# Attention with a projected sequence, then a maxout feed-forward layer: k of batch 1 turned by the DMA crossbar

## The chip, the cores and the metric

The kernel runs on one core of one Trainium2 chip. A core has five engines with instruction streams of their own: TensorE (PE in the profile; its weight loads are PEld), VectorE (DVE), ScalarE (ACT), GpSimd (POOL) and SyncE (SP). They share an on-chip buffer (SBUF), a buffer for matmul results (PSUM, eight banks of 512 fp32 values in each of 128 partitions) and 16 DMA engines. The metric is the device time of one execution in microseconds; the median of several runs is compared.

## The reference, cut to what matters

```python
# batch 8, heads 8, sequence 1024, head size 64, projected length 64
k_proj = np.einsum('ks,bhsd->bhkd', E, k)
v_proj = np.einsum('ks,bhsd->bhkd', F, v)
scores = np.matmul(q, k_proj.transpose(0, 1, 3, 2)) / 8
attn = np.exp(scores - max);  attn = attn / sum(attn)
x = np.matmul(attn, v_proj)            # then 8192 tokens x 512
h = np.maximum(np.maximum(x @ w1, x @ w2), x @ w3)    # 512 -> 768
out = h @ w_out                                      # 768 -> 512
```

The layer after the attention is most of the work: for each batch of 1024 tokens it has two chunks of 512 tokens, with 72 matmuls of 128x128 by 128x512 for the maxout and 24 for the way down.

## The kernel before

One instruction stream for each engine is written by hand as a list of steps. A step is one group of matmuls of the feed-forward layer: `l1` (four matmuls into one bank, for one of the three weights and one of six column blocks) or `down` (six matmuls into one bank). `at(slot, f)` puts a piece of the next batch's attention behind step `slot` of the present batch. Pieces run in the order in which they are listed, once their step is reached.

```python
def kv(b, bank=AB, crossbar=True):
    ...  # 8 + 8 matmuls: k projected into the lower half of the bank, v into the upper
    nc.scalar.copy(out=kp2[i][:, :, :, 0, :], in_=...)           # ScalarE
    nc.scalar.copy(out=vp2[b % 3][KP:P], in_=kv_v[:, 1])
    nc.vector.tensor_copy(out=kp_[:, :, 1:], in_=...)            # VectorE: three more copies of k
    nc.vector.tensor_copy(out=vp2[b % 3][0:KP], in_=kv_v[:, 0])
    if crossbar:
        nc.sync.dma_start_transpose(out=kpT[i]..., in_=kp2[i]...)

def kp_turn(b):                      # the same turn by TensorE, 16 transposes
    for h in range(H):
        for f in range(2):
            nc.tensor.transpose(out=psb[:, AB + h // 4, x:x + KP], ...)
    for j in range(2):
        (nc.vector.tensor_copy if j else nc.scalar.copy)(out=kpT[i][:, 4 * j:4 * j + 4]..., in_=psb[:, AB + j, ...])
```

`scores` takes `kpT` as weights and the turned q (`qT`, turned by VectorE in `q_flip`), and then gives two exponentials to ScalarE. The sums over the projected length and the product with v are small matmuls in quarter tiles (`quads`), each with two adjacent PSUM banks as its target. Banks 4 to 7 belong to the attention (`AB = 4`), banks 0 to 3 go round among the feed-forward groups (`fbank`). Some products borrow an adjacent pair from that ring (`fpair`).

```python
def sums(b):
    for ch in range(2):
        quads(b, ch, AB + 2 * ch, lambda rows, g: ones[rows, :])
    log(0)

def av3(b):
    lo = fpair()
    for f, ch, bank in ((0, 0, lo), (1, 0, AB), (0, 1, AB + 2)):
        av(b, f, ch, bank)
    norm(b, 0, 0, lo)

def av1(b):
    lo = fpair()
    av(b, 1, 1, lo)
    norm(b, 1, 1, lo)

def l1(b, ch, c, jt, i):
    bank = fbank()
    ...  # four matmuls
    if i == 0:   nc.scalar.copy(out=h1s[jt % 2], in_=ps[:, bank, :])                    # L225
    elif i == 1: nc.vector.tensor_tensor(out=m12[jt % 2], ..., in1=h1s[jt % 2], op=ALU.max)  # L227
    else:        nc.vector.tensor_tensor(out=hT[c % 2][:, jt, :], ..., in1=m12[jt % 2], op=ALU.max)  # L229

def load_behind_turn(b, order="qkv", q_of=None):
    nc.gpsimd.tensor_copy(out=seen, in_=kpT[(b - 1) % NB][:, 0, 0, 0:1])   # waits for the turn of batch b - 1
    ...
    for c in order:
        load(b, ...)
```

In the first two batches the pieces stand at these steps. Steps 17 to 34 of batch 0 are the 18 `l1` groups of chunk 1, steps 35 to 38 its four `down` groups; step 1 of batch 1 is the first `l1` of chunk 2.

```python
if b == 0:
    at(8, q_up0, slice(4, 8))
    for x in ((k, k_t), (v, v_t), (q, q_t)):
        at(18, load, 2, *x)
    at(22, kv, 1, AB, False)
    at(23, q_flip, 1, 0)
    at(24, q_flip, 1, 1)
    at(24, kp_turn, 1)
    at(26, scores, 1, 0)
    at(26, q_flip, 1, 2)
    at(27, q_flip, 1, 3)
    at(29, scores, 1, 1)
    at(32, sums, 1)
    ...
    at(35, av3, 1)
    at(36, norm, 1, 1, 0, AB)
    at(37, norm, 1, 0, 1, AB + 2)
elif b == 1:
    at(2, kv, 2)
    for g in range(4):
        at(4 + g, q_flip, 2, g)
    at(9, load_behind_turn, 3, "kvq")
    at(9, scores, 2, 0)
    at(12, scores, 2, 1)
    at(16, av1, 1)
    at(16, sums, 2)
    ...
```

Of the kernel before, what the change touches and what calls it, by code (L numbers as in the profile page):

```python
# [16 lines left out]
def kernel(ctx: ExitStack, tc: tile.TileContext, q, k, v, E, F, w1, w2, w3, w_out, out):  # L17
# [73 lines left out]
    def load_behind_turn(b, order="qkv", q_of=None):  # L91

        nc.gpsimd.tensor_copy(out=seen, in_=kpT[(b - 1) % NB][:, 0, 0, 0:1])
        if q_of:
            load(q_of, q, q_t)
        for c in order:
            load(b, *{"q": (q, q_t), "k": (k, k_t), "v": (v, v_t)}[c])
# [17 lines left out]
    AB = 4  # L115
    HD = D // 2

    def kv(b, bank=AB, crossbar=True):
        i = b % NB
        for si in range(SI):  # L120
            nc.tensor.matmul(out=ps[0:KP, bank, :], lhsT=eT[:, si, :], rhs=k_t[i][:, :, si, :],  # L121
                             start=(si == 0), stop=(si == SI - 1))
            nc.tensor.matmul(out=ps[KP:P, bank, :], lhsT=fT[:, si, :], rhs=v_t[i][:, :, si, :],  # L123
                             start=(si == 0), stop=(si == SI - 1))
        kp_ = kp2[i].rearrange("k h f r dd -> k (h f) r dd")
        kv_v = ps[KP:P, bank, :].rearrange("p (g u dd f) -> p u g f dd", u=2, f=2, dd=HD)
        nc.scalar.copy(out=kp2[i][:, :, :, 0, :], in_=ps[0:KP, bank, :].rearrange("p (h dd f) -> p h f dd", dd=HD, f=2))  # L127
        nc.scalar.copy(out=vp2[b % 3][KP:P], in_=kv_v[:, 1])
        nc.vector.tensor_copy(out=kp_[:, :, 1:], in_=kp_[:, :, 0:1].to_broadcast([KP, 2 * H, 3, HD]))  # L129
        nc.vector.tensor_copy(out=vp2[b % 3][0:KP], in_=kv_v[:, 0])  # L130
        if crossbar:
            nc.sync.dma_start_transpose(out=kpT[i].rearrange("p h f k -> p (h f) k"),
                                        in_=kp2[i].rearrange("k h f r dd -> k (h f r dd)"))

    def kp_turn(b):
        i = b % NB
        for h in range(H):
            for f in range(2):
                x = ((h % 4) * 2 + f) * KP
                nc.tensor.transpose(out=psb[:, AB + h // 4, x:x + KP], identity=ident[0:KP, 0:KP],  # L140
                                    in_=kp2[i][:, h, f].rearrange("k r dd -> k (r dd)"))
        for j in range(2):
            (nc.vector.tensor_copy if j else nc.scalar.copy)(
                out=kpT[i][:, 4 * j:4 * j + 4].rearrange("p h f k -> p (h f k)"), in_=psb[:, AB + j, 0:8 * KP])

    def scores(b, u):
        i = b % NB
# [21 lines left out]
            nc.tensor.matmul(out=ps[j * HD:(j + 1) * HD, bank + hh, :], lhsT=lhs(rows, g),  # L169
                             rhs=pT[b % NB][rows, g, ch, :], start=True, stop=True, tile_position=(u * KP, j * HD))  # L170

    def sums(b):
        for ch in range(2):
            quads(b, ch, AB + 2 * ch, lambda rows, g: ones[rows, :])
        log(0)

    def log(ch):
# [12 lines left out]

    def av3(b):
        lo = fpair()
        for f, ch, bank in ((0, 0, lo), (1, 0, AB), (0, 1, AB + 2)):
            av(b, f, ch, bank)
        norm(b, 0, 0, lo)

# [4 lines left out]


    ring = [0, 1, 2, 3]

    def fbank():
        ring.append(ring.pop(0))
# [24 lines left out]
    def down(b, ch, c, tt):  # L231
        o = o_acc[c % 2]
        if c == 2 * B - 1 and tt > 1:

            n = DO // 2
            for x in range(2):
                tmp = h1s[x] if tt == 3 else o[:, 2, x * n:(x + 1) * n]
                bank = fbank()
                for jt in range(NJT):
                    nc.tensor.matmul(out=ps[:, bank, :n], lhsT=hT[c % 2][:, jt, tt * P:(tt + 1) * P],  # L240
                                     rhs=wo_sb[:, jt, x * n:(x + 1) * n], start=(jt == 0), stop=(jt == NJT - 1))
                (nc.scalar.copy if x else nc.vector.tensor_copy)(out=tmp[:, :n], in_=ps[:, bank, :n])
                (nc.scalar if x else nc.sync).dma_start(out=out_v[b, ch][:, tt, x * n:(x + 1) * n], in_=tmp[:, :n])
            return
        bank = fbank()
        for jt in range(NJT):
            nc.tensor.matmul(out=ps[:, bank, :], lhsT=hT[c % 2][:, jt, tt * P:(tt + 1) * P],  # L247
                             rhs=wo_sb[:, jt, :], start=(jt == 0), stop=(jt == NJT - 1))
        nc.scalar.copy(out=o[:, tt, :], in_=ps[:, bank, :])  # L249
        if c == 2 * B - 1:  # L250
            nc.sync.dma_start(out=out_v[b, ch][:, tt, :], in_=o[:, tt, :])
        elif tt % 2 == 1:
            dst = out_v[b, ch] if b else out_0[ch]
            nc.gpsimd.dma_start(out=dst[:, tt - 1:tt + 1, :], in_=o[:, tt - 1:tt + 1, :])  # L254

    def down_half(tt, x):

# [245 lines left out]
    for b in range(B):  # L503
        n = b + 1
        groups = []

        def at(slot, f, *args):
            groups.append((slot, lambda: f(*args)))

        if b == 0:  # L510
            at(8, q_up0, slice(4, 8))
            for x in ((k, k_t), (v, v_t), (q, q_t)):
                at(18, load, 2, *x)
            at(22, kv, 1, AB, False)
            at(23, q_flip, 1, 0)
            at(24, q_flip, 1, 1)
            at(24, kp_turn, 1)
            at(26, scores, 1, 0)
            at(26, q_flip, 1, 2)
            at(27, q_flip, 1, 3)  # L520
            at(29, scores, 1, 1)
            at(32, sums, 1)
            at(32, log, 1)
            at(33, recip, 0)
            at(35, recip, 1)
            at(35, av3, 1)
            at(36, norm, 1, 1, 0, AB)
            at(37, norm, 1, 0, 1, AB + 2)
        elif b == 1:
            at(2, kv, 2)  # L530
            for g in range(4):
                at(4 + g, q_flip, 2, g)
            at(9, load_behind_turn, 3, "kvq")
            at(9, scores, 2, 0)
            at(12, scores, 2, 1)
            at(16, av1, 1)
            at(16, sums, 2)
            at(16, log, 1)
            at(17, recip, 0)
            at(19, recip, 1)  # L540
            at(24, load, 4, k, k_t)
            at(24, load, 4, v, v_t)
            at(25, av3, 2)
            at(26, norm, 2, 1, 0, AB)
            at(28, norm, 2, 0, 1, AB + 2)
            at(30, kv, 3)
            for g in range(4):
                at(32 + 2 * g, q_flip, 3, g)
        elif n < B:
            if b + 2 < B:  # L550
                at(3, lambda: kv(b + 2, fbank()))
            at(3, scores, n, 0)
            at(8, scores, n, 1)
            if b + 3 < B:
                at(11, load_behind_turn, b + 3, "qkv", 4 if b == 2 else None)
            at(14, av1, b)
            at(14, sums, n)
            at(14, log, 1)
            at(15, recip, 0)
            at(17, recip, 1)  # L560
            at(26, av3, n)
            at(27, norm, n, 1, 0, AB)
            at(29, norm, n, 0, 1, AB + 2)
            if b + 2 < B:
                for g in range(4):
                    at(33 + 2 * g, q_flip, b + 2, g)
        else:
            at(5, av1, b)
        slot = 0
        gi = 0  # L570

        def tick():
            nonlocal slot, gi
            slot += 1
            while gi < len(groups) and groups[gi][0] <= slot:
                groups[gi][1]()
                gi += 1

        for ch in range(2):
            c = 2 * b + ch  # L580
            if c == 0:
                for part in ((1, range(6), (6, 7, 0, 1, 4, 5)), (2, range(3), (2, 3, 0), lambda: q_up0(slice(0, 4))),
                             (2, range(3, 6), (1, 2, 3), scores_up0)):
                    for _ in l1_first(*part):
                        tick()
                ring[:] = [0, 1, 2, 3]
                for x in range(2):
                    if x:
                        av_up0()
                    for tt in range(4):  # L590
                        down_half(tt, x)
                        if x:
                            tick()
                        elif tt == 0:
                            sums0(1, 4)
                continue
            for s in range(18):
                l1(b, ch, c, s // 3, s % 3)
                tick()
                if pend and s in (2, 5, 8, 11):  # L600
                    pend.pop(0)()
                    tick()
            pend = [lambda tt=tt, b=b, ch=ch, c=c: down(b, ch, c, tt) for tt in range(4)]
        if b == 0:
            while pend:
                pend.pop(0)()
                tick()
# [32 lines left out]
```

## Time and profile before

| | |
|---|---|
| time, median of 3 runs | 396.37 us (395.94 to 396.93) |
| span of the profiled execution | 394.2 us |
| TensorE busy | 384.5 us, 98% |
| VectorE, ScalarE, GpSimd busy | 203.3, 162.7, 66.9 us |
| chain that ended last | 92% TensorE, 5% DMA |
| turn of k by the crossbar, six times | 4.1 us from issue to landing (median) |
| loads of k, q (512 KB each) | 13.6 and 12.2 us from issue to landing (median) |

The profile's times are microseconds from the start of the span. A row of the timeline names a run of equal instructions: start, duration, engine, line, operation, what it writes and reads, how many, and in brackets how long the engine sat idle before and what released it. A busy TensorE is not a TensorE at its peak, since matmuls overlap in the records: one 128x512 matmul is recorded with 0.38 us, while the next one starts much sooner. So costs on TensorE are read from starts, and not from durations. A few matmul records are missing, which shows as a count that is one short and a start that is one matmul late. DMA times to landing count from the issue by the engine to the completion.

### The profile page before, as it was taken

The numbers are of one execution on the slowest core, as the hardware profiler recorded it, in microseconds if no ns is written. First come the engines' busy times: TensorE is split into PE (matmuls) and PEld (weight loads), VectorE is DVE, ScalarE is ACT, GpSimd is POOL, SyncE is SP. The second block draws the span as 40 slices with busy tenths as digits, with TensorE's granted clock in tenths as the row PEclk, the third lists the DMA queues.
The fourth block names the chain that finished last, engine by engine and source line by source line (L and its number), as shares of the span: only waits on it lengthen the run. The fifth ranks groups of instructions, "written<-read, shape, count | busy, mean of one in ns | idle before, by whom it ended". The sixth has DMA issues, their size and how long they took to land.

```text
span 394.2 us, 6687 instructions
## 1 busy us (share of the span) xinstructions
PE 384.5 (98%) x2733; PEld 173.7 (44%) x2784; DVE 203.3 (52%) x304; ACT 162.7 (41%) x249; POOL 66.9 (17%) x109
## 2 busy tenths in 40 slices
PE   8999999999999999999999999999999999999996
PEld 4444444444444444444444444444444444444443
DVE  4447566655653476335763357525664456453342
ACT  4413467364326622455224732266234552222221
POOL 7452420162003400050000500000010000000000
PEclk9999999999999999999999999999999999999999
DMA  9999999499923995179611993131011111111023
GB/s 223 206 210 204 206 258 201 126 166 206 228 70 82 188 206 191 20 121 206 166 53 28 167 206 110 53 80 54 2 53 55 56 53 56 53 43 65 0 106 108
DMA packets 40398, 48.14 MB, mean 122 GB/s; under 512 B 8112, under 2 KB 35504, under 8 KB 40368
## 3 DMA queue, kind: packets, MB, share of 16 engines
q0 software_dynamic: 31792, 43.52, 53.2%
q1 hardware_dynamic: 7600, 3.15, 4.5%
q10 hardware_dynamic: 976, 1.05, 0.8%
q8 instruction: 22, 0.36, 0.4%
q14 instruction: 8, 0.07, 0.0%
HBM read 57.15 MB, written 16.78 MB: 188 GB/s over the span
## 4 chain that ended last, share of the span: by engine, by line
PE 92%; DMA 5%; issue 1%; ACT 1%; DVE 0%; POOL 0%; POOLq 0%; DVEq 0%
PE ps L222 59%; PE ps L247 19%; PE ps L121 3%; PE ps L169 3%; DMA w_sb<-in_moe_w_dram 3%; PE ps L462 2%; PE ps L155 2%; DMA k_t<-in_k_dram 2%; PE ps L260 1%; PE ps L453 1%; PE ps L240 1%; ACT pT L345 1%; PE ps L278 0%; POOL k_t L373 0%; PE ps L341 0%
## 5 line engine op out<-in xcount | busy, mean ns | idle before, releaser
L222 PE MATMUL ps<-xT,w_sb 128*128 128x512 bf16 x1049 | 242.8, 379 | 1.8 <-issue 0.2
L222 PEld LDWEIGHTS <-w_sb 128*128 128x128 bf16 x1080 | 103.5, 98 | 129.8 <-issue 8.4
L227 DVE TENSOR_TENSOR m<-ps,h1s 128x512 f32<-128x512 f32 x90 | 62.2, 691 | 134.5 <-PE ps L222 99.8
L247 PE MATMUL ps<-wo_sb,hT 128*128 128x512 bf16 x335 | 82.3, 379 | 0.5 <-issue 0.2
L225 ACT COPY h1s<-ps 128x512 f32<-128x512 f32 x90 | 53.0, 588 | 69.6 <-PE ps L222 69.2
L249 ACT COPY o_acc<-ps 128x512 f32<-128x512 f32 x58 | 34.0, 587 | 101.3 <-PE ps L247 85.8
L229 DVE TENSOR_TENSOR hT<-ps,m 128x512 bf16<-128x512 f32 x90 | 62.0, 689 | 8.1
L254 POOL DMA_DIRECT2D out_dram<-o_acc x28 | 15.2, 543 | 271.7 <-ACT o_acc L249 269.2
L247 PEld LDWEIGHTS <-hT 128*128 128x128 bf16 x348 | 33.5, 98 | 41.4 <-issue 1.9
L187 DVE TENSOR_TENSOR xT<-ps,rinv 128x1024 bf16<-128x1024 f32 x28 | 33.4, 1218 | 8.4 <-PE ps L169 8.4
L160 ACT ACTIVATE pT<-ps 128x1024 bf16<-128x1024 f32 x28 | 27.1, 1021 | 4.7 <-PE ps L155 4.4
L103 DVE STREAM_TRANSPOSE qT<-q_t 128x512 f32<-128x512 f32 x28 | 18.6, 689 | 0.0
L89 POOL DMA_DIRECT2D v_t<-in_v_dram x21 | 15.3, 745 | 10.5 <-DMA q_t<-in_q_dram 3.3
L178 ACT ACTIVATE lns<-ps 128x1024 f32<-128x1024 f32 x14 | 13.6, 1023 | 4.9 <-PE ps L169 4.9
L181 ACT ACTIVATE rinv<-lns 128x1024 f32<-128x1024 f32 x14 | 14.9, 1062 | 0.0
L121 PE MATMUL ps<-k_t,eT 128*64 128x512 bf16 x56 | 13.4, 382 | 0.0
L123 PE MATMUL ps<-v_t,fT 128*64 128x512 bf16 x56 | 13.4, 382 | 0.0
L127 ACT CAST kp<-ps 64x512 bf16<-64x512 f32 x7 | 4.1, 579 | 18.5 <-PE ps L123 18.5
L89 POOL DMA_DIRECT2D q_t<-in_q_dram x14 | 10.6, 768 | 4.3 <-DMA q_t<-in_q_dram 2.2
L89 POOL DMA_DIRECT2D k_t<-in_k_dram x14 | 10.6, 771 | 3.8 <-ACT o_acc L500 1.4
L462 PE MATMUL ps<-xT,w_sb 128*128 128x512 bf16 x46 | 10.6, 379 | 0.2 <-issue 0.2
L129 DVE COPY kp<-kp 64x1536 bf16<-64x1536 bf16 x7 | 3.9, 552 | 12.8 <-ACT kp L127 12.8
(92 smaller groups left out, 166.1 us busy)
## 6 DMA issues: line engine op xcount, KB each, us to landing
out_dram<-o_acc POOLq DMA_DIRECT2D x30, 512.0 KB, 3.0
k_t<-in_k_dram POOLq DMA_DIRECT2D x14, 512.0 KB, 13.6
q_t<-in_q_dram POOLq DMA_DIRECT2D x14, 512.0 KB, 12.2
v_t<-in_v_dram POOLq DMA_DIRECT2D x18, 256.0 KB, 15.4
v_t<-in_v_dram POOLq DMA_DIRECT2D x7, 512.0 KB, 15.7
w_sb<-in_moe_w_dram POOLq DMA_DIRECT2D x4, 384.0 KB, 10.2
k_t<-in_k_dram POOLq DMA_DIRECT2D x4, 256.0 KB, 8.0
w_sb<-in_moe_w_dram POOLq DMA_DIRECT2D x4, 192.0 KB, 9.9
```

The costliest lines, as they stand in the source:

```text
L89: nc.gpsimd.dma_start(out=dst[b % NB][:, slots], in_=sv[:, heads])
L103: nc.vector.transpose(out=qT[b % NB][:, hs].bitcast(FP32).rearrange("p h n -> p (h n)"), in_=q_t[b % NB][:, hs].rearrange("p h si d -> p ( ...
L121: nc.tensor.matmul(out=ps[0:KP, bank, :], lhsT=eT[:, si, :], rhs=k_t[i][:, :, si, :], start=(si == 0), stop=(si == SI - 1))
L160: nc.scalar.activation(out=pT[i][:, 2 * u + gg].rearrange("p ch (t r n) -> p r (ch t) n", t=4, r=4), in_=ps[:, AB:AB + 4, gg * 256:(gg + 1 ...
L187: nc.vector.tensor_tensor(out=xT[b % 2][:, f::2, ch, :], in0=ps[:, bank:bank + 2, :], in1=rinv[ch].rearrange("p (u n) -> p u n", u=2), op= ...
L222: nc.tensor.matmul(out=ps[:, bank, :], lhsT=w_sb[i][:, ct, jt * P:(jt + 1) * P], rhs=xT[b % 2][:, ct, ch, :], start=(ct == 0), stop=(ct == ...
L225: nc.scalar.copy(out=h1s[jt % 2], in_=ps[:, bank, :])
L227: nc.vector.tensor_tensor(out=m12[jt % 2], in0=ps[:, bank, :], in1=h1s[jt % 2], op=ALU.max)
L229: nc.vector.tensor_tensor(out=hT[c % 2][:, jt, :], in0=ps[:, bank, :], in1=m12[jt % 2], op=ALU.max)
L247: nc.tensor.matmul(out=ps[:, bank, :], lhsT=hT[c % 2][:, jt, tt * P:(tt + 1) * P], rhs=wo_sb[:, jt, :], start=(jt == 0), stop=(jt == NJT - 1))
L249: nc.scalar.copy(out=o[:, tt, :], in_=ps[:, bank, :])
L462: nc.tensor.matmul(out=ps[:, bank, :], lhsT=w_sb[i][:, ct, jt * P:(jt + 1) * P], rhs=xT[0][:, ct, 0, :], start=(ct == 0), stop=(ct == NCT ...
```

## The change

Batch 1's k was the only one of batches 1 to 7 that TensorE turned (batch 0 has a path of its own). The change gives that turn to the crossbar too, so that TensorE is spared its 16 transposes, and moves the groups that hang on it by two steps (scores 26 and 29 to 28 and 31, sums 32 to 34; av3 and the norms by one). Three things go with it:

- The loads of batch 2 are issued behind the turn of batch 1, in the order k, v, q, and not at step 18.
- The stores of chunk 1 are kept back and issued behind the turn of batch 2, ahead of the loads of batch 3.
- Where an attention group borrows banks from the ring, the part that uses the borrowed pair comes second: `av1` stands between the two halves of the sums, and in `av3` the product into banks 4 and 5 goes first. In batch 1 the scores of batch 2 move from steps 9 and 12 to 10 and 13.

```diff
     def load_behind_turn(b, order="qkv", q_of=None):
         nc.gpsimd.tensor_copy(out=seen, in_=kpT[(b - 1) % NB][:, 0, 0, 0:1])
+        while held and b == 3:
+            held.pop(0)()
...
-        if crossbar:
-            nc.sync.dma_start_transpose(...)
-    def kp_turn(b):
-        ...  (16 transposes and two copies)
+        nc.sync.dma_start_transpose(...)
...
-    def sums(b):
+    def sums(b, av_of=None):
         for ch in range(2):
             quads(b, ch, AB + 2 * ch, lambda rows, g: ones[rows, :])
+            if ch == 0 and av_of:
+                av1(av_of)
         log(0)
...
-        for f, ch, bank in ((0, 0, lo), (1, 0, AB), (0, 1, AB + 2)):
+        for f, ch, bank in ((1, 0, AB), (0, 0, lo), (0, 1, AB + 2)):
...
-            nc.gpsimd.dma_start(out=dst[:, tt - 1:tt + 1, :], in_=o[:, tt - 1:tt + 1, :])
+            put = lambda: nc.gpsimd.dma_start(out=dst[:, tt - 1:tt + 1, :], in_=o[:, tt - 1:tt + 1, :])
+            held.append(put) if c == 1 else put()
...
-            for x in ((k, k_t), (v, v_t), (q, q_t)):
-                at(18, load, 2, *x)
-            at(22, kv, 1, AB, False)
-            at(24, kp_turn, 1)                 (q_flip at 23, 24, 26, 27 as before)
-            at(26, scores, 1, 0)
-            at(29, scores, 1, 1)
-            at(32, sums, 1)
-            at(32, log, 1)
-            at(33, recip, 0)
+            at(22, kv, 1)
+            at(24, load_behind_turn, 2, "kvq")
+            at(28, scores, 1, 0)
+            at(31, scores, 1, 1)
+            at(34, sums, 1)
+            at(34, log, 1)
+            at(34, recip, 0)
             at(35, recip, 1)
-            at(35, av3, 1)
-            at(36, norm, 1, 1, 0, AB)
-            at(37, norm, 1, 0, 1, AB + 2)
+            at(36, av3, 1)
+            at(37, norm, 1, 1, 0, AB)
+            at(38, norm, 1, 0, 1, AB + 2)
...
-            at(9, scores, 2, 0)
-            at(12, scores, 2, 1)
-            at(16, av1, 1)
-            at(16, sums, 2)
+            at(10, scores, 2, 0)
+            at(13, scores, 2, 1)
+            at(16, sums, 2, 1)
...
-            at(14, av1, b)
-            at(14, sums, n)
+            at(14, sums, n, b)
```

More of the change, by code (lines that the diff above doesn't have):

```diff
@@ L116, with kv @@
     HD = D // 2
-    def kv(b, bank=AB, crossbar=True):
+    def kv(b, bank=AB):
         i = b % NB
@@ L130, in kv @@
         nc.vector.tensor_copy(out=vp2[b % 3][0:KP], in_=kv_v[:, 0])
-        if crossbar:
-            nc.sync.dma_start_transpose(out=kpT[i].rearrange("p h f k -> p (h f) k"),
-                                        in_=kp2[i].rearrange("k h f r dd -> k (h f r dd)"))
-    def kp_turn(b):
[L136 to L144, printed above, removed]
+        nc.sync.dma_start_transpose(out=kpT[i].rearrange("p h f k -> p (h f) k"),
+                                    in_=kp2[i].rearrange("k h f r dd -> k (h f r dd)"))
     def scores(b, u):
@@ L203 @@
     ring = [0, 1, 2, 3]
+    held = []
     def fbank():
@@ L511 @@
             at(8, q_up0, slice(4, 8))
-            for x in ((k, k_t), (v, v_t), (q, q_t)):
-                at(18, load, 2, *x)
-            at(22, kv, 1, AB, False)
-            at(23, q_flip, 1, 0)
-            at(24, q_flip, 1, 1)
-            at(24, kp_turn, 1)
-            at(26, scores, 1, 0)
-            at(26, q_flip, 1, 2)
-            at(27, q_flip, 1, 3)
-            at(29, scores, 1, 1)
-            at(32, sums, 1)
-            at(32, log, 1)
-            at(33, recip, 0)
+            at(22, kv, 1)
+            at(24, load_behind_turn, 2, "kvq")
+            for g, x in enumerate((23, 24, 26, 27)):
+                at(x, q_flip, 1, g)
+            at(28, scores, 1, 0)
[3 more added lines that the diff above has]
+            at(34, recip, 0)
             at(35, recip, 1)
-            at(35, av3, 1)
-            at(36, norm, 1, 1, 0, AB)
-            at(37, norm, 1, 0, 1, AB + 2)
+            at(36, av3, 1)
+            at(37, norm, 1, 1, 0, AB)
+            at(38, norm, 1, 0, 1, AB + 2)
         elif b == 1:
```

## The prediction

> **What bounds the kernel now.** I read the first part of the page first, then what TensorE waited for, and only then the stretches that the change touches, on the timeline.
>
> ```profile
> PE 384.5 (98%) x2733; PEld 173.7 (44%) x2784; DVE 203.3 (52%) x304; ACT 162.7 (41%) x249; POOL 66.9 (17%) x109
> ```
>
> TensorE is busy for 98% of the span at a granted clock of 1.000, and the chain that ended last is 92% TensorE. The other engines and the DMA matter only where they make TensorE wait. Its waits, longest first (columns: total us, times, longest), are nearly nothing:
>
> ```profile
> PE ps L358 <- DVE warm L362: 1.2, 1, 1.2
> PE ps L453 <- DMA w_sb<-in_moe_w_dram: 0.5, 1, 0.5
> PE ps L169 <- DVE hT L229: 0.5, 1, 0.5
> ```
>
> The first two lie in the first 21 us, which the change leaves alone. The third is the only long wait after 43 us. So the change can win only what it takes out of TensorE's own stream, plus about half a microsecond of waiting. The unit to count in is one step: four 128x512 matmuls. The chain has rows of 36 such matmuls in 7.77 us, which is 0.216 us each and **0.86 us a step**. A switch from full-array matmuls to small-tile ones adds 0.09: the row of 11 that starts at 58.06 and lasts 2.76 has its last start at 60.82 - 0.38 = 60.44, and the ones-matmuls start at 60.75, 0.31 later and not 0.216.
>
> The k turn of batch 1, TensorE's timeline (start, duration):
>
> ```profile
> 49.95 1.90 PE L222 MATMUL ps<-xT,w_sb 128*128 128x512 bf16 x7
> 51.78 0.64 PE L140 MATMUL ps<-ident,kp 64*128 64x64 bf16 x16
> 52.35 1.90 PE L222 MATMUL ps<-xT,w_sb 128*128 128x512 bf16 x8
> 54.18 0.66 PE L155 MATMUL ps<-qT,kpT 32*64 32x256 bf16 x32
> ```
>
> The x7 is two steps, eight matmuls, with one record lost. They end their share at 49.95 + 1.73 = 51.68, and the next step begins at 52.35, so the 16 transposes of 190 ns, which overlap, cost **0.67 us**.
>
> The one wait, timelines of TensorE, ScalarE and VectorE in batch 1's first chunk (brackets: idle before, and releaser):
>
> ```profile
> 82.80 3.63 PE L222 MATMUL ps<-xT,w_sb 128*128 128x512 bf16 x15
> 86.93 0.41 PE L169 MATMUL ps<-pT,vp 64*32 64x512 bf16 x8 [0.50 <-DVE hT L229]
> 82.94 1.94 ACT L160 ACTIVATE pT<-ps 128x1024 bf16<-128x1024 f32 x2 [0.86 <-PE ps L155]
> 84.76 0.59 ACT L225 COPY h1s<-ps 128x512 f32<-128x512 f32 x1
> 85.39 0.69 DVE L227 TENSOR_TENSOR m<-ps,h1s 128x512 f32<-128x512 f32 x1 [1.79 <-ACT h1s L225]
> 86.18 0.69 DVE L229 TENSOR_TENSOR hT<-ps,m 128x512 bf16<-128x512 f32 x1
> ```
>
> Two exponentials stand ahead of the h1s copy on ScalarE, so the copy starts 0.9 us after its matmuls (82.80 + 0.86 + 0.16), both maxima come late, and the last maximum holds a bank of the pair that av1 borrows next. 82.80 + 16 x 0.216 + 0.09 = 86.35 is when it could have started. It started at 86.93: **0.57 us** lost.
>
> **What the Trainium skill says.** "TensorE: Matmul & The Clock Gate", Part 4: PE-mode transpose, says that such a transpose is a matmul against an identity whose output lands in PSUM and needs a copy after it. The trace agrees: 0.67 us of TensorE, then copies of 0.59 us (ScalarE) and 0.38 us (VectorE). "DMA: Bandwidth & Descriptors", DMA Transpose (X-bar), says that the crossbar turns data on the DMA's write side and is issued from Sync or Scalar; here Sync issues it and no compute engine is used. The same page, Issuing engines are not separate DMA queues, says that DMAs of all issuers run on the same 16 DMA engines and interleave. So a turn can be slowed by transfers beside it; the stores of chunk 1 are held back for that. "Trainium Architecture — The Big Picture", Inside one NeuronCore, says that each engine follows its own stream and meets the others only at semaphores; the copy stuck behind the exponentials is that.
>
> **The change part by part.**
>
> *Crossbar for batch 1.* It removes 0.67 us from TensorE and two copies that were beside other work. It adds a transfer that has to land before the scores of batch 1, moved from step 26 to step 28. TensorE gets there at 49.95 + 6 x 0.863 + 0.09 = **55.23**. The turn cannot start before the VectorE copy that fills kp2 ends: 50.69 + 0.55 = 51.24, so it is issued at about 51.27. How long it takes depends on the buffer. The turns of even batches land 3.6, 3.5 and 3.5 us after issue, those of odd batches 4.9, 4.7 and 4.6. Two of them, in the view of the tile kpT, cut to a window each (start, then issue to landing):
>
> ```profile
> L132 SPq DMA_TRANSPOSE kpT<-kp x1: 1313/1313/1313, 74.1 to 74.1; - x1
> ...
> DMA to landing us min/median/max: 3.6/3.6/3.6
> ```
>
> ```profile
> L132 SPq DMA_TRANSPOSE kpT<-kp x1: 1242/1242/1242, 165.3 to 165.3; - x1
> ...
> DMA to landing us min/median/max: 4.7/4.7/4.7
> ```
>
> Batch 1 is odd. I choose 4.75: landing at about 56.0, and a **new wait of 0.8 us** (0.7 with 4.6, 1.0 with 4.9). The stores of chunk 0, going out at about 400 GB/s from 50 us, should be over near 53 and cross only its beginning.
>
> *Loads of batch 2 behind that turn.* They were issued from 44.45, now from about 56.5. After a turn the loads of batch 3 were issued at 78.26 and reached full rate only after 81.0 (rows: window, busy us by engine, granted clock, DMA share, GB/s):
>
> ```profile
> 79.00:80.00 1.00, 0.95 (x34) 0.56 (x36) 0.90 (x2) 0.34 (x1) 1.00 (x3) 1.00 0.19 22
> 80.00:81.00 1.00, 1.00 (x5) 0.45 (x5) 0.22 (x1) 1.00 (x2) 1.00 (x2) 1.00 0.67 66
> 81.00:82.00 1.00, 1.00 (x6) 0.39 (x4) 0.00 (x0) 1.00 (x2) 1.00 (x3) 1.00 1.22 207
> ```
>
> k and v are 2.10 MB in bf16. With 0.09 MB by 81.0 and 205 GB/s after, they take 2.7 + 9.8 = 12.5 us from issue, so they are there at about 69.0. The projection of batch 2 ran at 70.93 and will want them at about 71.1 (70.93 - 0.67 + 0.8). Hidden, 2 us to spare. q follows 5.1 us later, at 74.1; its first half is in by 71.6 and the q turns start near 75. Hidden, but with a small margin.
>
> *Batch 2's groups one step later, and the borrowed pair second.* In batch 1's first chunk a maxout triple is three steps, so steps 10 and 13 follow an h1s matmul group, where 9 and 12 followed the last of a triple. The h1s copy then precedes the exponentials and the delay is gone. Also, the sums of chunk 0 (one round of quads, 0.2 us) now precede av1, and the ring gives av1 an older pair. I take the whole **0.57**. At 96.06 av3 started 0.06 us late for the same reason (a 0.37 step and not 0.31): **0.06**. In the other batches the pair was free in time, so the new order earns nothing there.
>
> *The end of batch 0.* Scores at steps 28 and 31 now follow the last of a triple, so here the h1s copies fall behind exponentials. By the durations above the last maximum ends 4.7 us after the second scores began, and the first down needs it at 4.9: no wait. But the logs and reciprocals (1.94 and 1.06 us) now stand right in front of the down copies on ScalarE. With S the start of the sums: logs from S + 0.5, reciprocal to 3.4, copy of down 0 to 3.95, second reciprocal to 4.9, copy of down 1 to 5.4. Down 2 reuses down 0's bank at S + 4.03, down 3 reuses down 1's at S + 5.33. Cost **0.1**.
>
> *Stores of chunk 1 held.* 1 MB moves from about 68 to after the turn of batch 2, at 400 GB/s 2.6 us ahead of batch 3's loads. Those land near 94 (k, v), wanted at 102. Nothing.
>
> Sum: -0.67 - 0.57 - 0.06 + 0.8 + 0.1 = **-0.4 us**; 396.4 becomes 396.0.
>
> **The rivals.** (1) *The turn is in time*: on a DMA cleared of loads it takes 3.5, as the even ones do, and lands at 54.8. For it: the loads of batch 2 no longer run beside it. Against it: the odd turns at 165.3 and 258.2 ran with almost no load traffic and still took 4.7 and 4.6. It would give -1.2: 395.2. (2) *The loads become the bound*: if the turn or the ramp is 2 to 3 us slower than I took, the projection of batch 2 waits, or a q turn blocks VectorE and with it the maxima. For it: margins of 2 us and less. Against it: a late turn moves the deadline along with the load. It would give 397 to 398. (3) *The moved phase costs more*: copies behind the exponentials in batch 0 stall the bank ring. Four banks give about 1.5 us of slack there, and the same pattern in batch 1 lost only 0.57. It would give about 396.6.
>
> **Range and chances.** The three runs of before spread over 1.0 us. Rival 1 sets the lower end (395.2), rival 3 or a mild form of 2 the upper (396.8). No path leads to 8 us either way, so within 2% is nearly certain.
>
> **What would show it.** In the profile after: no small transposes by TensorE in 50 to 53 us; a wait of TensorE's scores or weight loads on the DMA of kpT near 55 us, of 0.7 to 1.0 (below 0.2: rival 1); a turn of batch 1 of 4.6 to 4.9 us to landing; no wait on hT before av1 near 87; no wait at the projection of batch 2; at most 0.2 before down 3. A gain over 1 us, or a wait on k_t, v_t or q_t after 60 us, would make me wrong.

## The result, and the profile after

| | before | after |
|---|---|---|
| median, beside each other (6 runs each) | 396.65 us | 394.85 us (394.49 to 395.89) |
| ratio, with its 95% interval | | 0.9962 [0.9945, 0.9980] |
| the same, measured a second time | 396.30 us | 394.88 us, 0.9968 [0.9956, 0.9981] |
| span of the profiled execution | 394.2 us | 393.1 us |

The change is worth 1.3 us by the second, narrower measurement. I had said 0.4, and the time lies below the range. First the engines, on the page of the changed kernel (its line numbers for these groups are six to ten smaller than before; L145 is the scores, L159 the quads, L215 the maxout, L240 the way down):

```profile
PE 387.7 (99%) x2768; PEld 173.2 (44%) x2768; DVE 202.5 (52%) x303; ACT 162.1 (41%) x248; POOL 67.0 (17%) x110
```

TensorE records more busy time than before (384.5) although it does less. The profile before had lost 51 matmul records (2784 weight loads, 2733 matmuls), this one has none missing. So busy time says nothing here, and starts do. What TensorE waited for, all of it (total us, times, longest):

```profile
PE ps L352 <- DVE warm L356: 1.2, 1, 1.2
PE ps L145 <- DMA kpT<-kp: 0.4, 1, 0.4
```

The wait on hT before the quads is gone, and one on the crossbar turn is new. Its place, on TensorE's timeline:

```profile
49.70 5.35 PE L215 MATMUL ps<-xT,w_sb 128*128 128x512 bf16 x24
55.46 0.66 PE L145 MATMUL ps<-qT,kpT 32*64 32x256 bf16 x32 [0.40 <-DMA kpT<-kp]
56.05 2.76 PE L215 MATMUL ps<-xT,w_sb 128*128 128x512 bf16 x12
```

Six steps run through without transposes. Without a wait the scores would have begun at 49.70 + 24 x 0.216 + 0.09 = 54.97; they began at 55.46, 0.49 us late. And the place of the old wait, on the timelines of TensorE, ScalarE and VectorE:

```profile
83.21 2.76 PE L215 MATMUL ps<-xT,w_sb 128*128 128x512 bf16 x12
85.91 0.41 PE L159 MATMUL ps<-pT,ones 64*32 64x512 bf16 x8
86.13 0.40 PE L159 MATMUL ps<-pT,vp 64*32 64x512 bf16 x8
82.73 0.58 ACT L218 COPY h1s<-ps 128x512 f32<-128x512 f32 x1 [0.72 <-PE ps L215]
83.35 1.94 ACT L150 ACTIVATE pT<-ps 128x1024 bf16<-128x1024 f32 x2
85.15 0.69 DVE L222 TENSOR_TENSOR hT<-ps,m 128x512 bf16<-128x512 f32 x1
```

The h1s copy now runs ahead of the two exponentials. The last maximum before the quads ends at 85.84, before TensorE gets there, and not 0.5 us after it. The sums of chunk 0 (8 ones-matmuls) come first, av1 (8 with vp) second.

A single profile cannot give the change as a difference of spans, since the time at which TensorE reaches batch 1's projection moves from run to run: from 47.85 to 48.86 us in the eleven profiles that have it at step 22, although TensorE's work up to there is the same in all. (The two latest, at 48.85 and 48.86, are also the two in which the full clock was first granted at 10.4 us; in the others it came at 3.9 to 6.5 us. No run tests whether that is the reason.) So I compare intervals between the starts of projections. They cut that away and stand alone for each part of the change:

| us from projection to projection | 1 to 2 | 2 to 3 | 3 to 4 |
|---|---|---|---|
| before | 22.83 | 31.19 | 13.61 |
| after, first profile | 22.62 | 30.57 | 13.61 |
| after, second profile | 22.15 | 30.56 | 13.61 |

The transposes are 22.83 - 22.15 = **0.68 us**, the waits at av1 and av3 are 31.19 - 30.57 = **0.62 us**, and the turn's wait is 22.62 - 22.15 = **0.47 us** in one profile and **nothing** in the other. After the third projection nothing differs by more than 0.05 us.

### The profile page after: what moved, and what is told of

Its sections match the earlier page's. It is cut to its first block, busy times and chain, and to the rows that moved or that the text cites. A ratio compares the mean times of both kernels' runs of the same rounds, so it can differ in the third digit from the quotient of the medians.

```text
span 393.1 us, 6707 instructions
## 1 busy us (share of the span) xinstructions
PE 387.7 (99%) x2768; PEld 173.2 (44%) x2768; DVE 202.5 (52%) x303; ACT 162.1 (41%) x248; POOL 67.0 (17%) x110
## 4 chain that ended last, share of the span: by engine, by line
PE 92%; DMA 6%; ACT 1%; POOL 0%; issue 0%; POOLq 0%
PE ps L215 59%; PE ps L240 19%; PE ps L123 3%; PE ps L159 3%; DMA w_sb<-in_moe_w_dram 3%; PE ps L456 2%; PE ps L145 2%; DMA k_t<-in_k_dram 2%; PE ps L254 1%; DMA kpT<-kp 1%; PE ps L447 1%; PE ps L233 1%; ACT pT L339 1%; PE ps L272 0%; POOL k_t L367 0%
## 5 line engine op out<-in xcount | busy, mean ns | idle before, releaser
L215 PE MATMUL ps<-xT,w_sb 128*128 128x512 bf16 x1080 | 244.3, 379 | 0.0
L215 PEld LDWEIGHTS <-w_sb 128*128 128x128 bf16 x1080 | 103.8, 98 | 129.7 <-issue 8.0
L240 PE MATMUL ps<-wo_sb,hT 128*128 128x512 bf16 x348 | 84.2, 379 | 0.0
L240 PEld LDWEIGHTS <-hT 128*128 128x128 bf16 x348 | 33.4, 98 | 41.5 <-issue 2.3
L456 PE MATMUL ps<-xT,w_sb 128*128 128x512 bf16 x48 | 10.9, 379 | 0.0
```

The lines of the kernel that those rows point to most:

```text
L215: nc.tensor.matmul(out=ps[:, bank, :], lhsT=w_sb[i][:, ct, jt * P:(jt + 1) * P], rhs=xT[b % 2][:, ct, ch, :], start=(ct == 0), stop=(ct == ...
L456: nc.tensor.matmul(out=ps[:, bank, :], lhsT=w_sb[i][:, ct, jt * P:(jt + 1) * P], rhs=xT[0][:, ct, 0, :], start=(ct == 0), stop=(ct == NCT ...
```

## The experiments

The theory from the first profile: the gain is the sum of the terms that the profile shows, -0.67 + 0.47 - 0.63. The rival: as the first measurement (ratio 0.9962, 1.5 us) was more than that sum of 0.8, something outside these terms was saved. Four kernels take the change apart.

**Crossbar alone.** The changed kernel with the order and the steps of batch 1 as before.

```diff
-        for f, ch, bank in ((1, 0, AB), (0, 0, lo), (0, 1, AB + 2)):
+        for f, ch, bank in ((0, 0, lo), (1, 0, AB), (0, 1, AB + 2)):
-            at(10, scores, 2, 0);  at(13, scores, 2, 1);  at(16, sums, 2, 1)
+            at(9, scores, 2, 0);   at(12, scores, 2, 1);  at(16, av1, 1);  at(16, sums, 2)
```

> Only the crossbar turn of batch 1, with its moved groups, the loads behind it and the held stores; the order of av1 and av3 and the steps 9 and 12 of batch 1 as before. Theory A (the change is the sum that its profile shows): -0.67 for the transposes and +0.47 for the wait on the turn, -0.2 us against before; the wait on hT before av1 near 87 is still there (0.5 to 0.6 us) unless the moved ring alone removes it. Theory B (the crossbar part saves something outside these terms, in the DMA or in the first 50 us): -0.8 us or more.

Measured: 395.52 us, ratio 0.9973 [0.9964, 0.9983], about -1.1 us, with intervals of 22.15 and 30.62. There was no wait on the turn here, and the wait near 87 was gone too, although the h1s copy still stood behind the exponentials: the last maximum ended at 86.96 and av1 began at 86.44. The other place of av3 in batch 0 had shifted the ring, so that av1 borrowed the banks of the 13th and 14th `l1` group of the chunk, and not those of the 14th and 15th. Theory A's -0.2 was too small by two terms that the trace shows: no wait on the turn (0.47), and the av1 wait removed by the ring (0.57). With them it is -1.25, as the two intervals say, and the time agrees within its interval. Theory B had the size of the time right, but named no term and isn't needed.

**Order alone**, on the kernel before: both new orders, and steps 10 and 13.

```diff
-            at(9, scores, 2, 0);   at(12, scores, 2, 1);  at(16, av1, 1);  at(16, sums, 2)
+            at(10, scores, 2, 0);  at(13, scores, 2, 1);  at(16, sums, 2, 1)
         (and the orders in sums and av3)
```

> Only the order (av1 between the sums, the borrowed pair second in av3) and the steps 10 and 13, on the kernel before with its TensorE turn. Theory A: -0.6 us, no wait before the quads near 87 and 96. Theory B: the same or less, as the rest of the 1.5 us came from the crossbar part.

Measured: 395.64 us, 0.9986 [0.9979, 0.9993], -0.55 us; intervals 22.84 and 30.56. As theory A had it; theory B allowed the same, so this run does not part them.

**Steps alone**, on the kernel before: only 10 and 13 for 9 and 12.

> Only the steps 10 and 13 in place of 9 and 12 in batch 1. If the copies behind the exponentials made the wait on hT: the wait of 0.5 us on hT near 87 is gone, -0.5 us. If it was the order of the borrowed pair: the wait stays at 0.3 us or more.

Measured: 395.78 us, 0.9986 [0.9980, 0.9993]; intervals 22.83 and 30.63. The wait on hT is gone. The copies behind the exponentials made it.

**Pair alone**, on the kernel before: only the orders in sums and av3.

> Only the order of the borrowed pair, steps 9 and 12 as before. One round of quads (0.2 us) now stands ahead of av1. If the late copy is the cause: the wait on hT shrinks from 0.57 to about 0.35 and does not go, -0.3 us with the 0.06 of av3. If the order alone was the cause: it is gone, -0.6 us.

Measured: 396.05 us, 0.9999 [0.9992, 1.0005]; intervals 22.83 and 30.94. The time doesn't show it, the trace does: 0.25 us of the 0.62, and among TensorE's waits this line is left:

```profile
PE ps L169 <- DVE hT L231: 0.2, 1, 0.2
```

So the wait at av1 has three cures, any of which works or helps: the steps (all of it), the ring shifted by the crossbar part (all of it), the pair's order (0.2 us, plus the 0.06 at av3). In the change they overlap, which is why the parts add up to more than the whole: by the intervals 1.25 and 0.63 us against 1.30. (The times, -1.07 and -0.55 against -1.3 to -1.5, point the same way, but their intervals are too wide to show it.) The next question was what sets the length of the turn.

**Loads beside the turn.** The changed kernel with the loads of batch 2 at step 18.

```diff
+            for x in ((k, k_t), (v, v_t), (q, q_t)):
+                at(18, load, 2, *x)
             at(22, kv, 1)
-            at(24, load_behind_turn, 2, "kvq")
```

> The changed kernel with the loads of batch 2 issued at step 18 again, so that they run beside the turn of batch 1. In the changed kernel the turn of batch 3 met 1.07 MB of other transfers and took 10.8 us. If transfers beside a turn hold it up: the turn of batch 1 lands 8 to 11 us after its issue and the scores wait 4 to 7 us, +4 to +6 us against the changed kernel. If the DMA engines share fairly: landing at 5 us or less, +0.5 us at most.

Measured: 404.84 us, 1.0213 [1.0191, 1.0235] against before. The turn in the view of the tile kpT (start, then issue to landing), TensorE's wait, and its timeline behind it:

```profile
L133 SPq DMA_TRANSPOSE kpT<-kp x1: 1933/1933/1933, 51.6 to 51.6; - x1
DMA to landing us min/median/max: 11.5/11.5/11.5
```

```profile
63.23 1.08 PE L145 MATMUL ps<-qT,kpT 32*64 32x256 bf16 x32 [7.56 <-DMA kpT<-kp]
64.24 3.80 PE L215 MATMUL ps<-xT,w_sb 128*128 128x512 bf16 x12
```

It is above the upper end of what I expected: 11.5 us and a wait of 7.56. The interval from projection 1 to 2 grew from 22.15 to 31.23, by 9.1 us. The wait is 7.6 of these; the 12 matmuls behind it took 3.80 in place of 2.76 us and the scores 1.08 in place of 0.66, which is the other 1.5. TensorE ran slower right after its long idle, and the granted clock accounts for it: half of the full one at first. Rows: window, busy us by engine, granted clock (third number from the end), DMA share, GB/s.

```profile
63.00:64.00 1.00, 0.77 (x32) 0.59 (x32) 0.00 (x0) 0.00 (x0) 0.00 (x0) 0.50 1.23 203
64.00:66.00 2.00, 2.00 (x21) 0.65 (x6) 0.00 (x0) 1.62 (x2) 0.00 (x0) 0.50 1.25 206
67.00:68.00 1.00, 1.00 (x13) 0.33 (x12) 0.69 (x1) 0.00 (x0) 0.00 (x0) 1.00 1.22 203
```

**Stores of chunk 1 at once.**

```diff
-            held.append(put) if c == 1 else put()
+            put()
```

> The changed kernel with the stores of chunk 1 issued at once. They then queue behind q of batch 2 and cross the turn of batch 2 (1 MB from about 73.5). If that turn is held up as the one of batch 3 was: landing at 6 to 8 us and not 3.5, at 80 to 81.5; the scores of batch 2 come at 79.3, so a new wait of 1 to 2 us. If it is not held up: no difference.

Measured: 394.82 us, 0.9967 [0.9957, 0.9976]: as the changed kernel. The turn of batch 2 met 0.12 MB and landed after 5.0 us: more than 3.5, less than the 6 to 8 that I expected. It landed at 79.22 and the scores came at 79.86, late enough to hide that. Holding the stores earns nothing measurable. It only moves the crossing: in the changed kernel the turn of batch 3 meets the delayed loads and stores (1.07 MB); with the stores issued at once it took 7.2 us. In the changed kernel:

```profile
L133 SPq DMA_TRANSPOSE kpT<-kp x1: 1243/1243/1243, 104.3 to 104.3; - x1
DMA to landing us min/median/max: 10.8/10.8/10.8
```

It lands at 115.1, and the scores of batch 3 begin at 116.50: 1.4 us to spare.

**Stores of chunk 0 held too**, until the turn of batch 1 has landed.

```diff
-        while held and b == 3:
+        while held and b in (2, 3):
...
-                nc.gpsimd.dma_start(out=out_0[0][...], in_=o_acc[0][...])
+                held.append(lambda: nc.gpsimd.dma_start(out=out_0[0][...], in_=o_acc[0][...]))
```

> The changed kernel with the stores of chunk 0 held back as well, until the turn of batch 1 has landed, so that this turn meets nothing from 50 us on. The turn took 4.4 us where the later ones took 3.5. If the stores crossing it (0.18 MB) were the cause: 3.5 us, the wait of 0.4 us on kpT goes, -0.5 us. If it is the issue by SyncE, which took 2.33 us in place of 1.24: landing stays at 4.4 and so does the wait.

Measured: 397.28 us, 1.0026 [1.0015, 1.0037] against before. The turn itself behaves as the first branch of the expectation said:

```profile
L133 SPq DMA_TRANSPOSE kpT<-kp x1: 1319/1319/1319, 51.2 to 51.2; - x1
DMA to landing us min/median/max: 3.6/3.6/3.6
```

The wait on kpT is gone and the interval to projection 2 is 22.15, with projection 1 at 48.00, nearly as early as in the first profile of the change (47.85). Landing after 4.4 us, the turn would have come at 55.57, after the 55.13 at which the scores began. So the stores made the turn longer there. (SyncE's issue row isn't the cause either: it was 2.3 us in the kernel with the crossbar alone, where the turn landed in 3.5.) But 1 MB of stores ahead of the loads made v of batch 2 late, which I had not expected of this run:

```profile
PE ps L125 <- DMA v_t<-in_v_dram: 2.3, 1, 2.3
```

**Projection of batch 1 at step 21.** One number changed.

> The changed kernel with the projection of batch 1 one step (0.86 us) earlier. v of batch 1 lands at about 47.0, and the step is at 47.0. If it has landed: the turn lands at about 54.6 and the wait on kpT goes, -0.47 us. If v is late: the wait moves to the projection and the gain is smaller.

Measured: 395.32 us, 0.9969 [0.9958, 0.9980]. The turn crossed 0.28 MB and took 4.6 us, but TensorE came one step later, and there was no wait on kpT or v_t. From projection 1 to 2 it is 23.01, that is 22.15 and the step. The wait is gone; the time shows no gain over the changed kernel, which fits a wait of 0.47 that arises in some executions only.

**The change once more.**

> The changed kernel once more, for a narrower interval. By the sum of the parts as the single changes measured them it is -0.67 (transposes) - 0.57 (wait on hT) - 0.06 (av3) + the wait on the turn, which is 0 when TensorE reaches the projection of batch 1 late and 0.5 when early: -0.8 to -1.3 us, ratio 0.9967 to 0.9980. If something unseen were in it, the first 1.5 us would hold: 0.9962 or below.

Measured: 394.88 us, 0.9968 [0.9956, 0.9981]. No wait on the turn in its profile: TensorE reached projection 1 at 48.20, the turn crossed 0.11 MB and took 3.9 us. -1.3 us is the sum without that wait, and nothing unseen is needed. The time alone would not exclude 0.9962. From projection 1 on the intervals do: they account for 1.31 us, and the rest of the program differs by 0.05 at most. Ahead of projection 1 a difference of 0.2 us could not be told from the start-up's spread of 1 us.

**Step 21 and free stores together.** 

> The changed kernel with the stores of chunk 1 not held and the projection of batch 1 at step 21: the wait on the turn of batch 1 cannot arise (TensorE comes 0.86 us later after the issue), and the turn of batch 3 no longer crosses 1 MB. No wait on kpT whatever the start; -1.3 us against before if all of it holds, so 0 to 0.5 us better than the changed kernel, not more.

Measured: 394.99 us, 0.9970 [0.9959, 0.9980]. No wait on kpT, though the turn of batch 1 took 4.6 us. It isn't faster than the changed kernel in any way that these runs can tell. I have no version that beats it.

**Buffers exchanged**, on the kernel before, for the basis of my largest wrong term.

```diff
-    kp2 = [T([KP, H, 2, 4, D // 2], BF16, f"kp2_{i}") for i in range(NB)]
+    kp2 = [T([KP, H, 2, 4, D // 2], BF16, f"kp2_{i}") for i in range(NB)][::-1]
         (and kpT in the same way)
```

> The kernel before with its two kp2 and its two kpT buffers exchanged, so that even batches use what odd ones used. In the kernel before the turns of batches 3, 5 and 7 took 4.6 to 4.9 us and the others 3.5, and the prediction put that down to the buffer. If it is the buffer: batches 2, 4 and 6 are now the slow ones (4.6), 3, 5 and 7 take 3.5. If it is the place in the order: as before. If it is the pair of both: no turn without crossing traffic is slow. The time does not change.

Measured: 396.24 us, 1.0001 [0.9992, 1.0010]. The slow turns stay with batches 3, 5 and 7 (4.9, 4.5, 4.6), the others take 3.5 and 3.6. Here is that of batch 5, which with the exchange uses the other buffer:

```profile
L132 SPq DMA_TRANSPOSE kpT<-kp x1: 1241/1241/1241, 165.4 to 165.4; - x1
DMA to landing us min/median/max: 4.5/4.5/4.5
```

It isn't the buffer. With seven turns in the program, those of batches 5 and 7 take 3.5 to 3.6, in the changed kernel as well.

The slow turns had traffic across them after all. That of batch 3 met 0.11 MB of the software queue in the kernel before (0.11 to 0.22 in all five programs with six turns, where it took 4.9 to 5.5 us). Those of batches 5 and 7 met one packet of the queue that the profile calls "instruction". Here is the turn of batch 5 from its first to its last packet, in the kernel before and in the changed one (queue, kind: packets, MB, busy share of the 16 DMA engines):

```profile
q1 hardware_dynamic: 1056, 0.26, 109.2%
q8 instruction: 1, 0.02, 2.3%
```

```profile
q1 hardware_dynamic: 1056, 0.26, 95.7%
```

The packet has 16 KB and takes 0.9 to 1.3 us. In the five programs with six turns it starts inside the turns of batches 5 and 7, all ten of which took 4.5 to 4.7 us. In the eight with seven turns it starts 0.2 to 0.7 us behind the turn's last packet, and all sixteen took 3.5 to 3.6. No run moved this packet alone, so the cause is not shown, but no turn of batches 5 and 7 falls outside the pattern.

## Why the prediction was wrong, step by step

- **Transposes, -0.67**: right. The intervals give 0.68.
- **The wait at av1 and the 0.06 at av3, -0.63**: right in size (0.62) and in cause, as the kernel with the steps alone shows. I did name the ring's older pair, but as part of the new order. It comes with the later av3 of the crossbar part, which by itself removes the wait at av1.
- **The new wait on the turn, +0.8**: this is the step that failed, with its sentence "How long it takes depends on the buffer". Its frame was right. I had 55.23 - 51.27 (the first is 55.22 when added up), so a turn of up to about 3.9 us costs nothing, and that is what the runs show: 3.9 gave no wait, 4.4 gave 0.47. The length that I put in, 4.75, was wrong. It came from "turns of odd batches are slow", a pattern of three against three in one program, with no mechanism behind it, and it fell with the exchanged buffers. The turns at 165.3 and 258.2, which I held against rival 1 as free of load traffic, each met the packet of the instruction queue. What the length follows is what crosses the turn. Of the turn of batch 1, with the software queue's bytes counted twice, from the turn's first packet to its last and from its issue to its landing:

| kernel | MB, first to last packet | MB, issue to landing | issue to landing, us | wait on kpT, us |
|---|---|---|---|---|
| stores of chunk 0 held | 0 | 0 | 3.6 | 0 |
| stores of chunk 1 at once | 0.02 | 0.23 | 3.6 | 0 |
| crossbar alone | 0.03 | 0.26 | 3.5 | 0 |
| after, second profile | 0.11 | 0.58 | 3.9 | 0 |
| after, first profile | 0.18 | 0.76 | 4.4 | 0.47 |
| step 21 and free stores | 0.30 | 0.82 | 4.6 | 0 (one step later) |
| step 21 | 0.28 | 0.88 | 4.6 | 0 (one step later) |
| loads beside the turn | 1.15 | 2.26 | 11.5 | 7.6 |

A longer turn also lets more cross it, so the table alone shows no cause; the runs that took the stores away and put the loads beside the turn do. One rival is left for part of it: a packet of the instruction queue also ran beside the turn's packets, for 0.05 us in the first profile after, 0.3 in the second and 0.6 to 0.7 with step 21, and holding the stores moved it away too. In the first profile, the one with the wait, that is too short to make the 0.6 us by which the turn's packets took longer there (2.43 us from first to last, against 1.84 with the stores held).

I had the stores "cross only its beginning" and priced that at nothing. They are the wait in the one profile of the changed kernel that has it. In the four profiles in which nothing up to this turn differs (two of the changed kernel, crossbar alone, stores of chunk 1 at once), the turn with TensorE early at projection 1 (47.85) meets 0.18 MB and is waited for, those with TensorE later (48.20, 48.85, 48.86) meet 0.11 to 0.02 MB and are not. The wait so takes back part of an early start.

- **The end of batch 0, +0.1**: wrong, it is nothing. Down 2 and down 3 follow each other without a break (12 matmuls in one row of 2.76 us). I had the copy of down 1 end 5.4 us after the start of the sums; it ended after 5.26 (66.70 + 0.59 - 62.03), just before down 3 needs the bank at 5.32.
- **Loads of batch 2 hidden**: right, with less room than I wrote. v landed at 58.9 + 10.9 = 69.8 and the projection began at 70.47: 0.7 us to spare and not 2. The run with the stores of chunk 0 held spent that and 2.3 us more.
- **Held stores worth nothing**: right, by the run without them.

Without the two wrong terms the sum is -1.3 us, and the measured ratio of 0.9968 of 396.30 is -1.3. Rival 1, the turn in time, had named 395.2, and I argued it down with the pattern of odd and even.

## What to carry to other kernels

A crossbar turn on the critical path took 3.5 us or more than three times that, by what was in flight beside it. So keep bulk transfers away by issuing them behind it, and size the wait from the bytes in flight (instruction packets too), not from a pattern in earlier landings. When two parts of a change each remove the same wait, their single gains add up to more than the whole, so look for the wait in the trace of each part. On a saturated engine compare starts between fixed points of the program, and not spans: the start-up varied by 1 us here, which is most of the gain.

## What the runs showed of the hardware that was not expected

- A crossbar turn that takes 3.5 us alone took 10.8 to 11.5 us with 1.1 to 1.2 MB of other transfers between its first and last packet. From issue to landing 2.0 to 2.3 MB of them went by, at 180 to 196 GB/s. The loads' own rate was 205, so they kept most of it, and the turn with its 0.26 MB got what was left. With the loads beside it, its first packet came 3.9 us after issue and not 1.2.
- After 7.56 us without work TensorE took 3.80 us for 12 matmuls that otherwise take 2.76, at a granted clock of 0.50 that became 1.00 between 66 and 67 us, some 3 us after it had begun to work again. The 2.25 us without work in the run with the stores of chunk 0 held left the clock at 1.00.
- One 16 KB packet of the instruction queue inside a crossbar turn of 0.26 MB went with 4.5 to 4.7 us to landing in ten of ten turns, and with none inside it was 3.5 to 3.6 in sixteen of sixteen.
